# A 128-row slot for one expert's last block that is at most half full; its outputs computed, scaled and scattered in two parts of columns

## The chip, the core and the metric

The kernel runs on one NeuronCore of one Trainium2 chip, with its five engines: TensorE (PE; its weight loads are listed apart as PEld), VectorE (DVE), ScalarE (ACT), GpSimd (POOL) and SyncE (SP, which here issues DMAs). The metric is the time of one execution on the device in microseconds; lower is better. Before the change three runs took 935.01, 935.73 and 935.83 us, a median of 935.73 us.

## What is computed

Attention over 8 batches, 8 heads, 576 positions and 64 features, then a mixture of 8 experts in which each of the 4608 tokens goes to exactly one expert:

```python
q_rot, k_rot = rotate(q), rotate(k)
attn = softmax(q_rot @ k_rot.T / sqrt(D))
x = (attn @ v).transpose(0, 2, 1, 3).reshape(4608, 512)

logits = x @ w_gate + modality_bias[modality_id]
e_idx = argmax(logits, axis=1)
gate_w = softmax(logits)[arange(N), e_idx]
for e in range(8):
    mask = e_idx == e
    h = relu(x[mask] @ w1[e])                    # w1[e]: 512 x 1024
    out[mask] = gate_w[mask, None] * (h @ w2[e]) # w2[e]: 1024 x 512
```

Which token goes where depends on the data. For the inputs of the reference the experts get 0, 1143, 0, 0, 0, 0, 2289 and 1176 tokens. In blocks of 256 that is 4 full blocks and 119 tokens for expert 1, 8 full blocks and 241 tokens for expert 6, 4 full blocks and 152 tokens for expert 7.

## The kernel before

The first half of the program is attention: 32 pairs of heads, software-pipelined by a table of times (`KEYS`, `AT`). After each batch the router (`route`) finds each token's expert and its place in that expert's list, and `scatter` writes token number and gate weight into a table in DRAM (`TAB`), 4608 rows for each expert and one empty region behind them. Rows that nobody writes hold the number `EMPTY`, which every later gather and scatter skips as out of bounds.

The second half works through **slots**. A slot is one block of 256 rows of one expert's list. Slots 0 to 7 hold full blocks found after five batches (`plan0`, into `PLA`); 11 more (`NB_STATIC`), slots 8 to 18, are planned after the last batch (`plan`, into `PLB`). In both plans entry 0 of a slot is the expert, entry 1 the first row in `TAB`, entry 2 whether the expert differs from that of the slot before. `plan` counts the blocks that remain for each expert (`nb`), and writes their sum to `TOT`. Behind the static slots stands `tc.If(tot > NB_STATIC)`, whose body runs all the other slots up to `NB_MAX` = 17; a run in which 11 slots are enough skips it.

For the inputs here the blocks stand as follows: slots 0 and 1 are expert 1, slots 2 to 6 expert 6, slot 7 expert 7, slots 8 to 10 expert 1 (slot 10 is the block with 119 tokens), slots 11 to 14 expert 6, slots 15 to 18 expert 7 (slot 18 is the block with 152 tokens). `nb` is 3, 4 and 4, so `TOT` is 11.

What one slot does, in the order in which `chain` writes it for PE, DVE, ACT and POOL, which keep that order:

- `m_plan`, `m_ix` (three slots ahead): SP reads the slot's plan entries into registers and loads the table's rows twice, as `ix` (for scatter and scale) and `xi` (for the gather).
- `m_rows` (two slots ahead): POOL works out `iy` and issues eight indirect DMAs, which gather the rows of x into `XG`; `t` is the half of the rows, `g` a quarter of the features.
- `m_load1`, `m_load2` (one slot ahead): SP loads w1 and w2 of the slot's expert into `ST1` and `ST2`, 2 MB each in four DMAs of 512 KB. They are conditional: where the expert doesn't change, nothing moves.
- `m_split`: ACT rounds a quarter of the weights to fp32r (`W1H`, `W2H`), DVE takes what is left over (`W1L`, `W2L`). This is done for every slot, loaded or not.
- `m_tr`, `m_tre`: DVE transposes the gathered rows in 32 by 32 blocks, ACT and DVE split them into `XTH` and `XTL` (both are parts of `HL`).
- `m_l1`: 96 matmuls of 256 columns in four groups, each followed by `m_l1e`: ACT's relu gives the high part `hh`, DVE the low part `hl`.
- `m_l2(s, t)`, once for each half of the rows: 24 matmuls of 512 columns into one PSUM bank, ACT scales them into `y` (two buffers), and POOL scatters the 128 rows of `y` to the output.

The last batch's routing and `plan` itself run inside the chain: `one()` takes one item from the list `late`, and is called ten times in a slot (four times behind the groups of `m_l1e`, twice behind `m_tre`, four times behind `m_split`), six times in slot 0. With 14 steps of `route`, 5 scatters and 7 items of `plan` with four steps each, the list ends with slot 2.

The scatters all write the tensor `out`, so the program makes each of them wait until the one before has landed.

Of the kernel before, what the change touches and what calls it, by code (L numbers as in the profile page):

```python
# [8 lines left out]
F32 = mybir.dt.float32  # L9
# [9 lines left out]
P = 128  # L19
# [6 lines left out]
NB_STATIC = 11  # L26
# [59 lines left out]
def tile_attention_moe(ctx: ExitStack, tc: tile.TileContext, qk, v, mod, wg, mb, w1, w2, rope, cf, ci, out):  # L86
# [19 lines left out]
    PLB = cst.tile([1, 3, NB_MAX], I32, name="PLB")  # L106
# [507 lines left out]
    def plan():  # L614
# [19 lines left out]
        t88 = t1("t88", [E, E])  # L634
        V_.tensor_tensor(t88, tri, nb.unsqueeze(1).to_broadcast([1, E, E]), op=ALU.mult)
# [20 lines left out]
        V_.tensor_scalar(pl[:, 2, 0:ns], ch, 0.0, None, op0=ALU.not_equal)  # L656
        yield
# [45 lines left out]
    slots = [(0, i) for i in range(NA)] + [(1, i) for i in range(NB_MAX)]  # L703
# [10 lines left out]
    def m_ix(s):  # L714
        d = ms[s]
        ix = d["ix"] = ixp.tile([P, 2, 2], I32, name="ix", tag="ix")
        i1 = nc.sync.dma_start(out=ix, in_=TAB[bass.ds(d["r"], BLK), :].rearrange("(p t) w -> p t w", t=2)).ins
# [12 lines left out]
    def m_gather(s, t, g, after=None):  # L730
        d = ms[s]
        if "iy" not in d:
            d["iy"] = ixp.tile([P, 8], I32, name="iy", tag="iy")
            nc.gpsimd.tensor_scalar(d["iy"], d["xi"][:, :, 0], 4.0, cview("I4"), op0=ALU.mult, op1=ALU.add)
        rows = (N if slots[s][0] else NPL * S) * 4
        inst = nc.gpsimd.indirect_dma_start(out=XG[s % 2][:, t, g, :], out_offset=None,  # L736
                                            in_=X.rearrange("n (i f) -> (n i) f", f=P)[0:rows],
                                            in_offset=bass.IndirectOffsetOnAxis(ap=d["iy"][:, 2 * g + t:2 * g + t + 1], axis=0),
                                            bounds_check=rows - 1, oob_is_err=False)
# [65 lines left out]
    def m_l1e(s, g):  # L805
        d = ms[s]
        ps = d["ps", g]
        sl = slice(g * 2, g * 2 + 2)
        nc.scalar.activation(d["hh"][:, sl, :], ps, AF.Relu)
        nc.vector.scalar_tensor_tensor(d["hl"][:, sl, :], ps, 0.0, d["hh"][:, sl, :].bitcast(F32), op0=ALU.max, op1=ALU.subtract)  # L810

    def m_l2(s, t):
        d = ms[s]
        ps = bank("Y")
        m = 0
        for c in range(8):
            for hx, w in ((d["hh"], W2[0]), (d["hl"], W2[0]), (d["hh"], W2[1])):
                nc.tensor.matmul(ps, hx[:, c, t * P:(t + 1) * P], w[:, c, :], start=(m == 0), stop=(m == 23))  # L818
                m += 1
        y = yp.tile([P, DM], F32, name="y", tag="y")  # L820
        nc.scalar.activation(y, ps, AF.Copy, scale=d["ix"][:, t, 1:2].bitcast(F32))  # L821
        nc.gpsimd.indirect_dma_start(out=out, out_offset=bass.IndirectOffsetOnAxis(ap=d["ix"][:, t, 0:1], axis=0),  # L822
                                     in_=y, in_offset=None, bounds_check=N - 1, oob_is_err=False)
# [37 lines left out]
    for n in range(NPAIR):  # L861
# [34 lines left out]
        if n % 4 == 3:  # L896
# [75 lines left out]
    def chain(lo, hi, begun):  # L972
# [6 lines left out]
        for s in range(lo, hi):  # L979
# [17 lines left out]
            if nxt:  # L997
                for t in range(2):
                    m_tr(s + 1, t)
                for t in range(2):  # L1000
# [11 lines left out]
            m_l2(s, 1)  # L1012
# [6 lines left out]
    ns = NA + NB_STATIC  # L1019
# [3 lines left out]
    with tc.If(tot > NB_STATIC):  # L1023
        prefetch(ns)
        chain(ns, NA + NB_MAX, False)
# [100 lines left out]
```

## Time and profile before

| | |
|---|---|
| median of three runs | 935.73 us |
| the profiled execution, its own time | 935.48 us |
| its span (first to last instruction) | 933.7 us |
| mean granted TensorE clock | 0.998 |
| SP issues the last batch's rows of x to DRAM (the end of attention) | 499.18 us |
| period of one slot (ACT's scaling of slot 17 at 902.76 us, of slot 16 at 880.31 us) | 22.45 us |

The page of a profile lists for each engine how long it was busy, then groups of equal instructions with their number and the mean time of one. The timeline lists instructions in order of time: start, duration, engine, line of the code, operation, output and input. What stands in brackets is how long the engine had been idle before, and whose end released it by the profile's inference. The stretches view gives each engine's busy time and the DMA rate between two times. All times count from the start of the span.

### The profile page before, as it was taken

Reading aid. Unit: us, or ns where it says so; the run is one execution under the profiler, and the core shown is the slowest. Engines: PE = TensorE matmul, PEld = TensorE weight load, DVE = VectorE, ACT = ScalarE, POOL = GpSimd, SP = SyncE. Lnnn points to the kernel's source line nnn. Section 1 sums busy time; section 2 is a strip of 40 time slices with the busy share of each in tenths; the row PEclk is TensorE's granted clock in tenths of the full one; section 3 lists DMA queues with packets and bytes.
Section 4 is the critical chain, followed back from the end, with each engine's and each line's share of the span. In section 5 each row is a group of like instructions: output and inputs, shape, how many; then the busy total and the mean of one; then the engine's idle time right before and its main releaser. Section 6 shows DMA issues by size and latency. Waiting matters only on the chain. (4 is left out here: it accounts for less than half of the span.)

```text
span 933.7 us, 24945 instructions
## 1 busy us (share of the span) xinstructions
PE 899.7 (96%) x9248; PEld 739.8 (79%) x9248; DVE 670.0 (72%) x1165; ACT 629.5 (67%) x1292; POOL 664.9 (71%) x498
## 2 busy tenths in 40 slices
PE   2999999999999999999999999999999999999996
PEld 2777777777777777777778888898889999999995
DVE  7577787777877778777886778666666666666661
ACT  2778787787878778787884665665555666665651
POOL 3988879898898988999933877776655666666400
PEclk9999999999999999999999999999999999999999
DMA  8856857677676775766752721117712511251100
GB/s 264 237 171 186 227 156 199 197 182 215 169 200 197 184 218 159 205 179 187 209 157 75 209 64 36 51 62 235 231 46 72 195 41 55 92 180 46 37 24 17
DMA packets 79292, 136.90 MB, mean 147 GB/s; under 512 B 28699, under 2 KB 50603, under 8 KB 78140
## 3 DMA queue, kind: packets, MB, share of 16 engines
q1 hardware_dynamic: 68460, 114.06, 43.5%
q0 software_dynamic: 9440, 19.46, 6.4%
q10 hardware_dynamic: 1264, 1.72, 0.6%
q8 instruction: 75, 1.23, 0.6%
q14 instruction: 53, 0.43, 0.2%
HBM read 140.59 MB, written 19.77 MB: 172 GB/s over the span
## 5 line engine op out<-in xcount | busy, mean ns | idle before, releaser
L330 ACT ACTIVATE P<-ps,mn 128x576 f32<-128x576 f32 x288 | 210.4, 737 | 91.2 <-DVE mn L323 91.0
L323 DVE TENSOR_REDUCE mn<-ps 128x1 f32<-128x576 f32 x288 | 204.0, 745 | 93.0 <-PE ps L314 52.7
L736 POOL DMA_INDIRECT XG<-X,iy x152 | 186.4, 1226 | 66.8 <-issue 49.7
L801 PE MATMUL psH<-HL,W1H 128*128 128x256 f32 x1152 | 204.1, 280 | 0.0
L314 PE MATMUL ps<-SW 64*128 64x288 f32 x960 | 166.8, 314 | 15.5 <-DMA SW<-HL 15.4
L801 PEld LDWEIGHTS psH<-HL,W1H 128*128 128x128 f32 x1152 | 177.3, 188 | 1.9 <-ACT W1H L274 0.5
L314 PE MATMUL ps<-HL 64*128 64x288 f32 x960 | 166.6, 313 | 0.9 <-ACT P L330 0.8
L801 PE MATMUL psH<-HL,W1L 128*128 128x256 f32 x576 | 161.6, 281 | 1.4 <-DVE W1L L271 1.4
L314 PEld LDWEIGHTS ps<-SW 64*128 64x128 f32 x960 | 134.9, 190 | 26.9 <-DMA SW<-HL 15.0
L314 PEld LDWEIGHTS ps<-HL 64*128 64x128 f32 x960 | 137.1, 190 | 22.2 <-issue 12.8
L271 DVE TENSOR_TENSOR W1L<-ST,W1H 128x1024 fp32r<-128x1024 f32 x76 | 90.2, 1223 | 80.2 <-ACT W1H L274 80.2
L392 PE MATMUL pa<-PH,V 128*64 128x320 f32 (+1 forms) x1024 | 138.3, 412 | 0.0
L822 POOL DMA_INDIRECT out_dram<-y,ix x38 | 40.5, 1067 | 126.1 <-ACT y L821 103.1
L818 PE MATMUL psY<-W2H,SW 128*128 128x512 f32 x304 | 121.2, 399 | 0.0
L818 PE MATMUL psY<-W2L,SW 128*128 128x512 f32 x304 | 119.8, 394 | 0.0
L336 PE MATMUL ps<-idf,P 64*128 64x64 f32 x2624 | 105.8, 230 | 7.3 <-ACT P L330 1.8
L336 PEld LDWEIGHTS ps<-idf,P 64*128 64x128 f32 x2624 | 92.9, 141 | 22.3 <-ACT PH L274 9.0
L801 PEld LDWEIGHTS psH<-HL,W1L 128*128 128x128 f32 x576 | 108.4, 188 | 1.8 <-DVE W1L L271 1.8
L291 POOL TENSOR_TENSOR HL<-ST,HL 128x1216 fp32r<-128x1216 f32 x31 | 86.1, 2776 | 32.7 <-ACT HL L274 32.5
L392 PEld LDWEIGHTS pa<-PH,V 128*64 128x64 f32 x1024 | 67.9, 136 | 48.4 <-issue 10.0
L368 DVE COPY PH<-ps 128x512 f32<-128x512 f32 (+1 forms) x160 | 96.1, 633 | 8.6 <-PE ps L336 8.0
L271 DVE TENSOR_TENSOR W2L<-ST,W2H 128x1024 fp32r<-128x1024 f32 x76 | 92.6, 1219 | 4.5 <-ACT W2H L274 4.4
(173 smaller groups left out, 1585.4 us busy)
## 6 DMA issues: line engine op xcount, KB each, us to landing
ST<-in_moe_w_dram SPq DMA_DIRECT2D x152, 512.0 KB
ST<-in_qk_dram SPq DMA_DIRECT2D x62, 608.0 KB
SW<-HL SPq DMA_DIRECT2D x124, 232.0 KB
V<-in_v_dram SPq DMA_DIRECT2D x32, 256.0 KB
X<-X SPq DMA_DIRECT2D x8, 1024.0 KB
XG<-X,iy POOLq DMA_INDIRECT x152, 3.2
V<-in_v_dram SPq DMA_DIRECT2D x64, 16.0 KB
X<-XT SPq DMA_DIRECT2D x16, 64.0 KB
```

What stands on the lines that cost most here:

```text
L271: nc.vector.tensor_tensor(o, a, b, op=ALU.subtract)
L291: e.tensor_tensor(d["HL"][:, 1, c], a, d["HL"][:, 0, c].bitcast(F32), op=ALU.subtract)
L314: free(nc.tensor.matmul(ps[:, g, 0:288], t[:, wq, q0:q0 + P], t[:, wk, k0:k0 + 288], start=(m == 0), stop=(m == len(L) - 1)), seen)
L323: lastmin[d["ring", u]] = nc.vector.tensor_reduce(mn, d["S", u][:, :, 0:288], op=ALU.min, axis=AX.XY).ins
L330: nc.scalar.activation(p.rearrange("p (a b) -> p a b", a=2), ps[:, :, 0:288], AF.Exp, bias=d.pop(("m", u)), scale=-1.0, accum_out=d["sum"] ...
L336: free(nc.tensor.transpose(ps[0][:, g, c:c + 64], src[r, k0:k0 + P], idf[r, r]), ps[1])
L368: mine.append((nc.vector.tensor_copy if g else acopy)(o, i).ins)
L392: i = nc.tensor.matmul(pa[hh * 64:hh * 64 + 64, 0:c1 - c0], d["V"][:, hh, kt, :], r, start=(kt == 0), stop=(kt == 4))
L736: inst = nc.gpsimd.indirect_dma_start(out=XG[s % 2][:, t, g, :], out_offset=None, in_=X.rearrange("n (i f) -> (n i) f", f=P)[0:rows], in_o ...
L801: l1_[s] = nc.tensor.matmul(ps[:, i, :], w[:, c, f0:f0 + P], x[:, c, :], start=(m == 0), stop=(m == 11)).ins
L818: nc.tensor.matmul(ps, hx[:, c, t * P:(t + 1) * P], w[:, c, :], start=(m == 0), stop=(m == 23))
L822: nc.gpsimd.indirect_dma_start(out=out, out_offset=bass.IndirectOffsetOnAxis(ap=d["ix"][:, t, 0:1], axis=0), in_=y, in_offset=None, bounds ...
```

## The change

One of the eleven later slots is replaced by a slot of 128 rows. `plan` looks for the first expert whose last block has at most 128 tokens, takes that block out of its `nb`, and writes its place into an 18th entry of `PLB`. If there is none, that entry points at the table's empty region. The short slot stands behind the first ten later slots and in front of the `If`, whose bound becomes 10. The number of static slots is 19 as before. For the inputs here slots 8 and 9 are now expert 1, 10 to 13 expert 6, 14 to 17 expert 7, and slot 18 is the short one, with the 119 tokens of expert 1.

In the short slot only the first half of the rows (`t` = 0) is gathered, transposed and split; `m_l1` still runs with 256 columns, of which the second 128 are left from slot 17 and aren't used; `m_l1e` evaluates 128 columns. `m_l2` runs once, in two parts of 256 columns each with 24 matmuls; each part has its own PSUM bank, its own `y` and its own scatter into half rows of `out`, at row numbers `ho` that POOL works out ahead. `late` gets 13 items of `plan` in place of 7. The weights of the short slot, and of the slot that follows it in the `If`, are always loaded.

```diff
-NB_STATIC = 11
+NB_STATIC = 10
...
+    PLB = cst.tile([1, 3, NB_MAX + 1], I32, name="PLB")
...
+        V_.tensor_scalar(ni, nf, float(BLK // 2 - 1), None, op0=ALU.add)
...
+        V_.tensor_tensor(hm, nb, hm, op=ALU.subtract)
...
+        V_.tensor_scalar(hc, hc, 1.0, None, op0=ALU.is_equal)
...
+        V_.tensor_tensor(nb, nb, hm, op=ALU.subtract)
...
+        V_.tensor_copy(pl[:, 1, ns:ns + 1], hr)
...
+        V_.tensor_copy(pl[:, 0, ns:ns + 1], hr)
...
+        V_.memset(pl[:, 2, ns:ns + 1], 1)
...
+        V_.memset(pl[:, 2, NB_STATIC:NB_STATIC + 1], 1)
...
+    slots = [(0, i) for i in range(NA)] + [(1, i) for i in range(NB_STATIC)] + [(2, NB_MAX)] + [(1, i) for i in range(NB_STATIC, NB_MAX)]
+    halves = lambda s: range(1 if slots[s][0] == 2 else 2)
...
+            n = 4 * len(halves(s))
+            nc.gpsimd.tensor_scalar(d["iy"][:, 0:n], d["xi"][:, 0:n, 0], 4.0, cview("I4"), op0=ALU.mult, op1=ALU.add)
+            if n == 4:
+                ho = d["ho"] = ixp.tile([P, 2], I32, name="ho", tag="ho", bufs=1)
+                for h in range(2):
+                    nc.gpsimd.tensor_scalar(ho[:, h:h + 1], d["ix"][:, 0, 0:1], 2.0, float(h), op0=ALU.mult, op1=ALU.add)
...
-        for t in range(2):
+        for t in halves(s):
...
+        n = P * len(halves(s))
+        hh, hl = (d[x][:, g * 2:g * 2 + 2, 0:n] for x in ("hh", "hl"))
+        nc.scalar.activation(hh, ps[:, :, 0:n], AF.Relu)
...
+        nh = 2 if slots[s][0] == 2 else 1
+        w = DM // nh
+        for h in range(nh):
+            ps = bank("Y")[:, 0:w]
...
+                    nc.tensor.matmul(ps, hx[:, c, t * P:(t + 1) * P], x[:, c, h * w:h * w + w], start=(m == 0), stop=(m == 23))
...
+            nc.scalar.activation(y[:, 0:w], ps, AF.Copy, scale=gate)
+            row = d["ho"][:, h:h + 1] if nh > 1 else d["ix"][:, t, 0:1]
+            nc.gpsimd.indirect_dma_start(out=out.rearrange("n (i f) -> (n i) f", f=w) if nh > 1 else out,
...
-                late = steps + scats + [(each, next) + ((g, None),) * 4] * 7
+                late = steps + scats + [(each, next) + ((g, None),) * 4] * 13
...
-            m_l2(s, 1)
+            if len(halves(s)) > 1:
+                m_l2(s, 1)
...
-    ns = NA + NB_STATIC
+    ns = NA + NB_STATIC + 1
```

Two places in the order of instructions matter below. The first is the end of POOL's program in front of the `If`: the scatters of slot 17 (first two rows) and of slot 18, with the semaphores that each waits for. `DMASW`, with a number, is one of eight semaphores that count landed DMAs of POOL, taken in turn. Before:

```order
L822 DMA out_0_dram<-y_13269,ix_12433 4608x512 [waits DMASW7_49,DMAHW0_49,DMASW0_49,Activation_49]
L822 DMA out_0_dram<-y_13303,ix_12433 4608x512 [waits DMASW1_49,DMASW0_49,Activation_49]
L822 DMA out_0_dram<-y_13453,ix_12688 4608x512 [waits DMASW2_49,DMAHW2_49,DMASW1_49,Activation_49]
L822 DMA out_0_dram<-y_13483,ix_12688 4608x512 [waits DMASW3_49,DMASW2_49,Activation_49]
L1022 TENSOR_LOAD TOT_79 [waits DVE_49]
L1023 COMPARE_AND_BRANCH
```

And now, with the two half-row scatters (9216 rows of 256) in the third and fourth row:

```order
L895 DMA out_0_dram<-y_13284,ix_12460 4608x512 [waits DMAHW0_49,DMASW3_49,Activation_49]
L895 DMA out_0_dram<-y_13318,ix_12460 4608x512 [waits DMASW4_49,Activation_49]
L895 DMA out_0_dram<-y_13468,ho_12919 9216x256 [waits DMASW5_49,DMASW6_49,Activation_49,Pool_49]
L895 DMA out_0_dram<-y_13498,ho_12919 9216x256 [waits DMASW6_49,DMASW7_49,Activation_49,Pool_49]
L1097 TENSOR_LOAD TOT_79 [waits DVE_49]
L1098 COMPARE_AND_BRANCH
```

Each scatter still waits for the semaphore of the scatter before it: the second half's wait for `DMASW6` is for the landing of the first half.

The second place is DVE in slot 3, from the third group of the first layer to the transposes for slot 4 (`HL_82` is `hl`). Before:

```order
L271 TENSOR_TENSOR W2L<-ST_74,W2H 128x1024 [waits DMAHW0_49,Activation_49]
L810 SCALAR_TENSOR_TENSOR HL_82<-psH,SW_84 128x512 [waits Activation_49]
L271 TENSOR_TENSOR W2L<-ST_74,W2H 128x1024 [waits DMAHW1_49,Activation_49]
L810 SCALAR_TENSOR_TENSOR HL_82<-psH,SW_84 128x512 [waits Activation_49]
L781 STREAM_TRANSPOSE XG_75<-XG_75 128x512 [waits DMASW2_49,DMASW7_49,DMASW1_49,DMASW0_49]
```

And now:

```order
L877 SCALAR_TENSOR_TENSOR HL_82<-psH,SW_84 128x512 [waits Activation_49]
L709 MEMSET PLB 1x1 [waits DVE_49]
L714 TENSOR_SCALAR ge<-nb 1x8
L717 TENSOR_SCALAR fa<-AB 1x8
L719 TENSOR_TENSOR ge<-ge,fa 1x8 [waits DVE_49]
L271 TENSOR_TENSOR W2L<-ST_74,W2H 128x1024 [waits DMAHW1_49,Activation_49]
L877 SCALAR_TENSOR_TENSOR HL_82<-psH,SW_84 128x512 [waits Activation_49]
L721 TENSOR_TENSOR ge<-ge,fa 1x7 [waits DVE_49]
L723 TENSOR_TENSOR cmp<-cmp,ge 1x136 [waits DVE_49]
L726 TENSOR_REDUCE rb<-cmp 1x17 [waits DVE_49]
L729 TENSOR_SCALAR r_9773<-CF 1x17
L847 STREAM_TRANSPOSE XG_75<-XG_75 128x512 [waits DMASW2_49,DMASW7_49,DMASW1_49,DMASW0_49]
```

The rest of `plan` follows six items of `late` later than before: its old places in slot 2, between the parts of `W1L`, are taken by the new instructions on the short block, and behind the groups of slot 3 stand 22 small instructions where there were none (5, 5, 4 and 4 behind the four `hl`, 4 behind the transposes).

More of the change, by code (lines that the diff above doesn't have):

```diff
@@ L105, in tile_attention_moe @@
     PLA = cst.tile([1, 3, NB_MAX], I32, name="PLA")
-    PLB = cst.tile([1, 3, NB_MAX], I32, name="PLB")
+    PLB = cst.tile([1, 3, NB_MAX + 1], I32, name="PLB")
     TOT = cst.tile([1, 1], I32, name="TOT")
@@ L656, in plan @@
         V_.tensor_scalar(pl[:, 2, 0:ns], ch, 0.0, None, op0=ALU.not_equal)
+        yield
+        V_.memset(pl[:, 2, NB_STATIC:NB_STATIC + 1], 1)
         yield
@@ L701, in bank @@
         return spare.pop()
-    slots = [(0, i) for i in range(NA)] + [(1, i) for i in range(NB_MAX)]
+    slots = [(0, i) for i in range(NA)] + [(1, i) for i in range(NB_STATIC)] + [(2, NB_MAX)] + [(1, i) for i in range(NB_STATIC, NB_MAX)]
+    halves = lambda s: range(1 if slots[s][0] == 2 else 2)
     ms = {}
@@ L716, in m_ix @@
         ix = d["ix"] = ixp.tile([P, 2, 2], I32, name="ix", tag="ix")
+        if slots[s][0] == 2:
+            nc.sync.dma_start(out=ix[:, 0, :], in_=TAB[bass.ds(d["r"], P), :])
+            xi = d["xi"] = ixp.tile([P, 8, 2], I32, name="xi", tag="xi")
+            nc.sync.dma_start(out=xi[:, 0:4, :], in_=TAB[bass.ds(d["r"], P), :].rearrange("(q g) w -> q (g w)", g=4).unsqueeze(0).to_broadcast([4, 32, 8]))
+            return
         i1 = nc.sync.dma_start(out=ix, in_=TAB[bass.ds(d["r"], BLK), :].rearrange("(p t) w -> p t w", t=2)).ins
@@ L997, in chain @@
             if nxt:
-                for t in range(2):
+                for t in halves(s + 1):
                     m_tr(s + 1, t)
-                for t in range(2):
+                for t in halves(s + 1):
                     m_tre(s + 1, t)
@@ L1024, in tile_attention_moe @@
         prefetch(ns)
-        chain(ns, NA + NB_MAX, False)
+        chain(ns, len(slots), False)
 CF_OFF = {}
```

68 lines of the change are left out of this document (53 added, 15 removed).

## Prediction, made before the result was known

> **What bounds the kernel now.** I read the page first, then the stretches of the last two slots, then the timeline of their engines.
>
> ```profile
> span 933.7 us, 24945 instructions
> PE 899.7 (96%) x9248; PEld 739.8 (79%) x9248; DVE 670.0 (72%) x1165; ACT 629.5 (67%) x1292; POOL 664.9 (71%) x498
> ```
>
> ```profile
> 880.30:902.70 22.40, 22.40 (x146) 20.23 (x145) 15.26 (x16) 13.29 (x16) 1.96 (x2) 1.00 0.07 25
> 902.70:925.10 22.40, 22.40 (x144) 19.91 (x143) 9.58 (x10) 9.34 (x12) 1.95 (x2) 1.00 0.06 21
> ```
>
> In slots 17 and 18 (columns behind the stretch: its length, then PE, PEld, DVE, ACT, POOL busy, clock, DMA share, GB/s) PE is busy for all 22.4 us, at full granted clock (1.00), while the others rest a third of the time or more. But a busy PE isn't yet a price, because matmuls overlap. The price is the distance between starts. PE in slot 18, first and last matmul of each layer:
>
> ```profile
> 902.51 0.28 PE L801 MATMUL psH<-HL,W1H 128*128 128x256 f32 x1
> ...
> 913.66 0.28 PE L801 MATMUL psH<-HL,W1L 128*128 128x256 f32 x1
> 913.77 0.39 PE L818 MATMUL psY<-W2H,SW 128*128 128x512 f32 x1
> ...
> 924.73 0.40 PE L818 MATMUL psY<-W2L,SW 128*128 128x512 f32 x1
> ```
>
> The 96 matmuls of 256 columns take (913.66 - 902.51) / 95 = 0.1174 us each, the 48 of 512 columns (924.73 - 913.77) / 47 = 0.2332 us. So time goes by columns: half as many cost half. Behind the last matmul only a tail remains:
>
> ```profile
> 925.22 0.69 ACT L821 ACTIVATE y<-psY,ix 128x512 f32<-128x512 f32 x1 [4.92 <-PE psY L818]
> 926.18 0.97 POOL L822 DMA_INDIRECT out_dram<-y,ix  x1 [4.63 <-ACT y L821]
> ```
>
> ACT starts 0.49 us behind the last matmul's start, POOL 0.27 us behind ACT's end (925.91); POOL ends at 927.15, and landing, branch and the program's end take the 6.55 us to 933.7. So what ends last is PE, then this tail.
>
> **The change, part by part.**
>
> *Does the short slot get used?* Only if one of the experts leaves at most 128 rows. Counted from the reference, expert 1 leaves 119. The trace agrees: both scatters of slot 10 (from 741.23 and 746.55 us) and the last of slot 18 show, in the DMA view of their stretches:
>
> ```profile
> q0 software_dynamic: 80, 0.12, 6.7%
> ...
> q0 software_dynamic: 80, 0.12, 6.6%
> ...
> q0 software_dynamic: 80, 0.16, 5.2%
> ```
>
> 0.12 MB is 60 rows of 2 KB in each half, 119 or 120 in the block; 0.16 MB is 76 and so 152. `TOT` becomes 10, the bound is 10, and the body of the `If` stays skipped.
>
> *Layer 2 of the last slot.* Two parts of 24 matmuls with 256 columns. The operands have the shape of those in layer 1, so I take 0.1174 us. From the start at 913.77, the last matmul of part 0 starts at 913.77 + 23 x 0.1174 = 916.47, that of part 1 at 913.77 + 47 x 0.1174 = 919.29, against 924.73: **-5.44 us**. Part 0's `hl` isn't late either. DVE's last one, at the old size:
>
> ```profile
> 914.60 0.69 DVE L810 SCALAR_TENSOR_TENSOR HX<-psH,SW 128x512 fp32r<-128x512 f32 x1 [0.64 <-ACT SW L809]
> ```
>
> It is done at 915.29, and now it is half as wide; its first user, the 20th matmul of part 0, starts at 913.77 + 19 x 0.1174 = 916.00.
>
> *Scale.* 128x256 from PSUM by the same ACT operation:
>
> ```profile
> L274 ACT ACTIVATE oT<-pa 128x256 f32<-128x256 f32 x32 | 12.2, 382 | 0.1
> ```
>
> 0.38 us in place of 0.69. The 0.49 us from a matmul's start to ACT shrinks with the matmul's shown time (0.40 to 0.28), to 0.37. Part 0 is scaled from 916.84 to 917.22, part 1 from 919.66 to 920.04: a further -0.43 us.
>
> *Scatters.* POOL could take part 0 at 917.49 (till 918.46) and part 1 at 920.31. But part 1 waits for the landing of part 0. The nearest rows are those where y had long been ready: slot 4's second y, scattered in the last row below.
>
> ```profile
> 610.87 0.69 ACT L821 ACTIVATE y<-psY,ix 128x512 f32<-128x512 f32 x1 [3.02 <-PE psY L818]
> ...
> 618.94 1.45 POOL L822 DMA_INDIRECT out_dram<-y,ix  x1 [0.30 <-issue]
> 622.91 0.99 POOL L822 DMA_INDIRECT out_dram<-y,ix  x1 [2.53 <-ACT SW L809]
> ...
> 635.68 1.41 POOL L822 DMA_INDIRECT out_dram<-y,ix  x1 [0.30 <-issue]
> 641.78 1.03 POOL L822 DMA_INDIRECT out_dram<-y,ix  x1 [4.69 <-DVE HX L810]
> ```
>
> y was done at 611.56, POOL stood idle for 2.53 us, so the named ACT instruction isn't the cause; the landing is. In the second pair, while weights are loading, it is 4.69 us. At the end of the kernel DMA is quiet (21 GB/s above), so I take 2.53: part 1 starts at 918.46 + 2.53 = 920.99 and not at 920.31, **+0.68 us**. Bounds: 0 (landing in time) and +2.84 us (4.69). What waits behind it is only POOL's load of `TOT`, the branch and the end. Ending at 920.99 + 0.97 = 921.96, plus 6.55 us, the span is 928.51.
>
> The Trainium skill ("DMA: Bandwidth & Descriptors", Anatomy of one DMA) gives a POOL DMA about 2.0 us of fixed time, mostly the receipt of the write, plus bytes over 436 GB/s. It speaks against cutting one output in two, since here the fixed part is paid in series. By it part 0 (0.12 MB) would land 2.28 us after its issue, and part 1 would start at 920.74: 0.25 us earlier than by the row.
>
> *New work on DVE in slot 3.* PE needs `hl` there in time: the fourth one when its 20th matmul of layer 2 starts (last row).
>
> ```profile
> 565.37 0.15 DVE L668 TENSOR_TENSOR ge<-ge,fa 1x7 f32<-1x7 f32 x1
> 565.55 0.29 DVE L670 TENSOR_TENSOR cmp<-cmp,ge 1x136 f32<-1x136 f32 x1
> 565.87 0.28 DVE L673 TENSOR_REDUCE rb<-cmp 1x17 f32<-1x136 f32 x1
> 566.08 0.21 DVE L676 TENSOR_SCALAR r<-CF 1x17 f32<-1x17 f32 x1
> ```
>
> ```profile
> 571.63 0.67 DVE L810 SCALAR_TENSOR_TENSOR HL<-psH,SW 128x512 fp32r<-128x512 f32 x1
> ...
> 575.94 1.23 DVE L271 TENSOR_TENSOR W2L<-ST,W2H 128x1024 fp32r<-128x1024 f32 x1 [0.16 <-ACT W2H L274]
> 577.80 0.69 DVE L810 SCALAR_TENSOR_TENSOR HL<-psH,SW 128x512 fp32r<-128x512 f32 x1 [0.64 <-ACT SW L809]
> ```
>
> ```profile
> 581.40 0.39 PE L818 MATMUL psY<-W2H,HL 128*128 128x512 f32 x1
> ```
>
> 14 small instructions now stand between the first `hl` and the fourth. They start 0.18 to 0.32 us apart, some 0.2 on average: 2.8 us, less 0.80 us of idle time that they fill, so the fourth `hl` ends at 578.49 + 2.0 = 580.5, before 581.40: cost **nothing**, with 0.9 us to spare. At 0.32 each it ends at 582.2, 0.8 us late; that is the upper bound, and nothing behind it (transposes, `XTL`, `W1L`) has less room.
>
> *A sixth set of weights.* Slot 18 now loads expert 1's 4.2 MB, which slot 18 of before didn't. The nearest case is slot 15, loaded from 810.27; DMA by stretches (last column GB/s):
>
> ```profile
> 810.27 7.11 SPq L752 DMA_DIRECT2D ST<-in_moe_w_dram  x4
> ...
> 877.63 6.80 SPq L752 DMA_DIRECT2D ST<-in_moe_w_dram  x4
> ```
>
> ```profile
> 815.00:820.00 5.00, 5.00 (x45) 5.00 (x45) 5.00 (x6) 4.38 (x6) 4.42 (x3) 1.00 0.76 249
> 820.00:825.00 5.00, 5.00 (x41) 4.83 (x40) 3.71 (x5) 2.22 (x4) 4.08 (x4) 1.00 0.94 297
> 825.00:830.00 5.00, 5.00 (x23) 4.02 (x22) 3.78 (x5) 2.07 (x2) 3.39 (x4) 1.00 0.77 259
> 830.00:835.00 5.00, 5.00 (x23) 4.02 (x22) 2.36 (x2) 2.58 (x3) 1.01 (x1) 1.00 0.18 64
> ```
>
> All of it has landed some 20 us after the first issue, w1, issued first, in the first half of that, and PE never waited. For slot 18 that is 877.6 to 898. ACT first reads the two here:
>
> ```profile
> 897.75 2.00 ACT L274 ACTIVATE W1H<-ST 128x1024 fp32r<-128x1024 f32 x2
> ...
> 905.24 1.05 ACT L274 ACTIVATE W2H<-ST 128x1024 fp32r<-128x1024 f32 x1
> ```
>
> That is 20 us behind the first issue for w1 and 28 us for w2. Cost: **nothing**. If it were late, PE would wait for the whole of it beyond the some 2 us that lie between the split of w1's first quarter and 902.51.
>
> *Dropped with the second half:* four gathers, one transpose, one split in slots 16 and 17, all beside a busy PE: nothing. The two `ho` and the narrower `iy` stand on POOL in slot 16 in place of four gathers of 1.0 us or more.
>
> **Sum**: -5.44 - 0.43 + 0.68 = -5.19 us, from 935.48 (profiled execution; the runs' median is 0.25 higher) to **930.3 us**. For comparison: one part of 512 columns would give -24 x 0.2332 = -5.60 us, so cutting in two loses 0.4 us as I see it.
>
> **Rivals.**
>
> 1. *The second scatter doesn't wait*, since part 0 lands by 920.3. For it: smaller rows. Against: 2.53 us was the least in a quiet stretch. Time 929.6. Chance 0.10.
> 2. *The small DVE instructions hold up PE* in slot 3 by up to 0.8 us: 931.1. For it: DVE has next to no gap between the first `hl` and the fourth. Against: 0.9 us of room. Chance 0.08.
> 3. *Narrow matmuls are bound by their weight loads.* Each load takes 188 ns:
>
> ```profile
> L801 PEld LDWEIGHTS psH<-HL,W1H 128*128 128x128 f32 x1152 | 177.3, 188 | 1.9 <-ACT W1H L274 0.5
> ```
>
> If loads came one after the other, part 1's last matmul would start at 913.77 + 47 x 0.188 = 922.61, POOL would end at 924.60, and the time would be 932.9. Against: layer 1 has the same loads and runs at 0.117. The Trainium skill ("TensorE: Matmul & The Clock Gate", Back-to-back issue gap) says that in a stream of pairs of load and matmul the spacing is set by both, 81 ns at 128 columns and 131 ns at 512, so that half the columns is not half the time. An estimate on the line between its two figures is 98 ns at 256 columns, three quarters of 131, by which layer 2 here would save a quarter of 11.2 us, 2.8 us, and not 5.4. The trace disagrees: 117 against 233 ns. Chance 0.03.
>
> 4. *Slower: the `If` is taken.* It decides at 128 tokens: with 129 in the last block of expert 1 no short block is found, `TOT` stays 11, and 11 > 10 sends the program through all seven slots of the body, 7 x 22.4 = 157 us, behind a load of w1 that nothing hides (some 10 us): about 1097. Against: 119, from two sides. Chance 0.02.
> 5. *No change*: w1 of slot 18 lands some 27 us after its issue (20 to ACT's read, 2 of room, 5.2 that eat up the gain) in place of 20 or less: 935.5. Against: PE's busy share of 22.40 in 22.40 us in slots behind such loads. Chance 0.03; 0.01 for worse.
>
> **How the numbers follow.** The forecast has 0.73: 930.3. The range takes in rivals 1 and 2 and most of the scatter's bounds: 929.2 to 932.4. A measurement can tell about 0.2%, 1.9 us, from no change: faster 0.94 (forecast and rivals 1 to 3), same 0.03, slower 0.03.
>
> **What would show it.** Right: 48 matmuls of 256 columns 0.117 us apart in the last slot; two scatters of about 1 us with POOL idle some 2.5 us between them, the second y done 0.7 us before the second scatter; PE without idle time from slot 3 on. Wrong: idle PE around 581 us (rival 2) or in front of slot 18's matmuls (5); a spacing near 0.19 (3); work behind the branch (4).

## The result and the profile after

| kernel | us, median (runs, range) | ratio to before, 95% interval |
|---|---|---|
| before | 935.37 (4, 934.90 to 935.83) | |
| after | 928.76 (4, 927.24 to 931.42) | 0.9925 [0.9906, 0.9943] |
| forecast | 930.3 (929.2 to 932.4) | 0.9945 |

The change makes the kernel 6.6 us faster; 5.2 were forecast, and the median lies 0.4 us below the range. The profiled execution of after took 931.42 us (span 929.5), the slowest of its four. First the page of after and the stretches of slots 17 and 18 (columns as before):

```profile
span 929.5 us, 24955 instructions
PE 891.4 (96%) x9248; PEld 733.8 (79%) x9248; DVE 672.8 (72%) x1187; ACT 626.9 (67%) x1291; POOL 664.3 (71%) x496
```

```profile
880.90:903.30 22.40, 22.40 (x146) 20.22 (x145) 13.64 (x14) 12.34 (x15) 1.95 (x2) 1.00 0.59 192
903.30:920.50 17.20, 17.20 (x146) 16.96 (x144) 8.55 (x10) 8.27 (x12) 1.93 (x2) 1.00 0.03 11
```

PE is busy in all of 17.20 us of the short slot, where slot 18 of before had 22.40, and the sixth set of weights (192 GB/s in slot 17) costs it nothing. The timeline of after's end, in three pieces, from slot 17's second scaling; then first and last matmul of layer 2:

```profile
903.71 0.69 ACT L893 ACTIVATE y<-psY,ix 128x512 f32<-128x512 f32 x1 [3.01 <-issue]
917.75 0.47 ACT L893 ACTIVATE y<-psY,ix 128x256 f32<-128x256 f32 x1 [2.50 <-PE psY L890]
920.60 0.47 ACT L893 ACTIVATE y<-psY,ix 128x256 f32<-128x256 f32 x1 [2.37 <-PE psY L890]
```

```profile
918.99 0.97 POOL L895 DMA_INDIRECT out_dram<-y,ho  x1 [13.35 <-ACT y L893]
922.80 0.97 POOL L895 DMA_INDIRECT out_dram<-y,ho  x1 [2.84 <-DMA out_dram<-y,ho]
```

```profile
914.66 0.28 PE L890 MATMUL psY<-W2H,SW 128*128 128x256 f32 x1
...
920.23 0.28 PE L890 MATMUL psY<-W2L,SW 128*128 128x256 f32 x1
```

The 48 matmuls stand (920.23 - 914.66) / 47 = 0.1185 us apart (forecast 0.1174). The first scatter starts 0.77 us behind its scaling (917.75 + 0.47 to 918.99), where 0.27 was forecast, and the second waits for the landing. The chain of waits shows how (start, duration, what; POOLq is POOL's sequencer):

```profile
918.99 2.95 DMA out_dram<-y,ho
...
921.97 0.02 POOLq L895
921.99 0.04 issue
922.03 0.04 POOLq L895
922.07 0.52 issue
922.59 0.50 POOLq L1097
```

The landing takes 2.95 us from the first scatter's start. Two short entries of POOL's sequencer follow (921.97, 922.03), and then 0.52 us in which, as we read it, the second scatter is set up.

Where the rest came from is seen further ahead. First matmul of layer 2 in slots 0, 2, 4 and 17, before and then after:

```profile
506.89 0.39 PE L818 MATMUL psY<-W2H,SW 128*128 128x512 f32 x1
...
554.52 0.39 PE L818 MATMUL psY<-W2H,SW 128*128 128x512 f32 x1
...
599.43 0.39 PE L818 MATMUL psY<-W2H,SW 128*128 128x512 f32 x1
...
891.32 0.39 PE L818 MATMUL psY<-W2H,SW 128*128 128x512 f32 x1
```

```profile
509.57 0.40 PE L890 MATMUL psY<-W2H,SW 128*128 128x512 f32 x1
...
556.27 0.40 PE L890 MATMUL psY<-W2H,SW 128*128 128x512 f32 x1
...
601.07 0.40 PE L890 MATMUL psY<-W2H,SW 128*128 128x512 f32 x1
...
892.26 0.40 PE L890 MATMUL psY<-W2H,SW 128*128 128x512 f32 x1
```

From slot 4 to slot 17 before takes 291.89 us, after 291.19: 22.45 and 22.40 us a slot, though PE runs the same instructions there and waits for nothing. From slot 0 to slot 4 before takes 92.54, after 91.50. Neither was in the forecast. Against it, slot 0's layer 2 starts 2.68 us later in this execution; in ten profiles taken on the first chips, of either kernel, that start lies anywhere from 506.4 to 510.0 us, so a single execution says little of a change of 1 us.

The chips of the last two batches were slower for all kernels (before took 940 to 945 us there), and single executions stalled at odd places, so from those runs only distances within one stage are compared, and the ratios (not the medians) of small_pad and after_dense leave out one slow run each.

### The profile page after: what moved, and what is told of

Read it like the earlier page. It is cut to its first block, busy times and chain, and to the rows that moved or that the text cites. A ratio compares the mean times of both kernels' runs of the same rounds, so it can differ in the third digit from the quotient of the medians.

```text
span 929.5 us, 24955 instructions
## 1 busy us (share of the span) xinstructions
PE 891.4 (96%) x9248; PEld 733.8 (79%) x9248; DVE 672.8 (72%) x1187; ACT 626.9 (67%) x1291; POOL 664.3 (71%) x496
## 4 chain that ended last, share of the span: by engine, by line
PE 65%; ACT 15%; DVE 8%; issue 6%; DMA 2%; POOL 2%; SPq 1%; DVEq 0%; POOLq 0%; ACTq 0%
PE psH L867 20%; PE psY L890 20%; ACT P L330 13%; PE ps L314 11%; PE pa L392 8%; DVE mn L323 6%; PE ps L336 6%; ACT PH L274 1%; POOL XG L802 1%; DMA SW<-HL 1%; DMA XG<-X,iy 1%; DVE ST L287 1%; DMA ST<-in_qk_dram 0%; PE pa L424 0%; DMA out_dram<-y,ho 0%
## 5 line engine op out<-in xcount | busy, mean ns | idle before, releaser
L895 POOL DMA_INDIRECT out_dram<-y,ix x36 | 44.5, 1236 | 105.1 <-ACT y L893 58.1
L890 PE MATMUL psY<-W2H,SW 128*128 128x512 f32 (+1 forms) x304 | 118.8, 391 | 0.0
L890 PE MATMUL psY<-W2L,SW 128*128 128x512 f32 (+1 forms) x304 | 118.2, 389 | 0.0
L271 DVE TENSOR_TENSOR W2L<-ST,W2H 128x1024 fp32r<-128x1024 f32 x76 | 92.5, 1218 | 4.7 <-ACT W2H L274 4.6
```

What stands on the lines that cost most here:

```text
L271: nc.vector.tensor_tensor(o, a, b, op=ALU.subtract)
L890: nc.tensor.matmul(ps, hx[:, c, t * P:(t + 1) * P], x[:, c, h * w:h * w + w], start=(m == 0), stop=(m == 23))
L895: nc.gpsimd.indirect_dma_start(out=out.rearrange("n (i f) -> (n i) f", f=w) if nh > 1 else out, out_offset=bass.IndirectOffsetOnAxis(ap=ro ...
```

## The experiments

In this table "0 to 4" and "4 to 17" are the distances of the layer-2 starts of those slots, "end" the distance from slot 17's second scaling to the end of the trace, all in us from the profiled execution; the time is the median.

| kernel | time | ratio to before | 0 to 4 | 4 to 17 | end |
|---|---|---|---|---|---|
| before | 935.37 | | 92.5 | 291.9 | 30.9 |
| before_again | 936.06 | 0.9999 [0.9983, 1.0014] | 92.3 | 292.0 | 30.9 |
| after | 928.76 | 0.9925 [0.9906, 0.9943] | 91.5 | 291.2 | 25.8 |
| after_again | 929.92 | 0.9934 [0.9911, 0.9957] | 91.6 | 291.2 | 26.2 |
| one_part | 929.55 | 0.9928 [0.9901, 0.9954] | 91.4 | 291.2 | 24.6 |
| parts_nowait | 929.43 | 0.9933 [0.9915, 0.9952] | 91.7 | 291.2 | 26.2 |
| pad128 | 936.05 | 0.9985 [0.9971, 1.0000] | 92.8 | 291.2 | 31.2 |
| after_unshift | 931.73 | 0.9943 [0.9922, 0.9963] | 91.9 | 291.9 | 26.5 |
| one_narrow | 928.57 | 0.9905 [0.9885, 0.9925] | 91.5 | 291.2 | 24.1 |

**The same kernels again.**

> The kernel before, unchanged, for the spread of one kernel and for the parts of its span. Theory A (the size of the gain lies in the start): attention begins 1.7 to 2.9 us earlier or later from one execution to the next, whatever the kernel, so the time against the other copy of the kernel before is within 0.3%, the period of a slot is 22.45 us as in the first profile, and the start (27th exponential, 41.81 us before) may differ by 1 to 3 us. Theory B (the change makes the expert stage itself faster): the period is again 22.45 us and the first slots are as before, within 0.1 us.

> The changed kernel, unchanged. Theory A: ratio 0.9925 to 0.9945 to the kernel before (5 to 7 us faster); from the end of slot 17 on the profile repeats the first one of this kernel (second scatter 3.8 us after the first, 0.7 us or more of it waiting), the 27th exponential is earlier than 43.55 us, and the slots' period follows the chip, so that it equals that of the copy of the kernel before run beside it. Theory B: the period is 22.40 us again while the copy of the kernel before has 22.45 us, and slots 1 to 3 take 1 us less.

The end (30.9 against 25.8 and 26.2) and the slot period come out the same each time: after_again has 22.40 us where before_again, on the same chip, has 22.45, so theory B holds for the period, and theory A's guess that it follows the chip falls. Theory B's "first slots as before, within 0.1 us" was missed: from slot 0 to slot 2 the same kernel took 47.6 us in before and 46.9 in before_again. The time itself spreads by 4 to 6 us among executions of one kernel; the median of after_again, 929.92 us, lies inside the forecast range. What a part of the change is worth is therefore read from distances inside the profile.

**The place of the weights.** The change adds four small tiles (`hm`, `hc`, `hr`, `ho`). In the program's layout they push `W1H`, `W1L`, `W2L` and `y` 128 bytes higher. pad128 does that to before, after_unshift undoes it in after; no instruction is added or taken away:

```diff
-full = t1("full", [E, NB_MAX])[:, :, 0:most]
+full = t1("full", [E, NB_MAX + 4])[:, :, 0:most]   # pad128, in before
+full = t1("full", [E, NB_MAX - 4])[:, :, 0:most]   # after_unshift, in after
```

> The kernel before; only a scratch tile of plan0 (full) is made 128 bytes longer, so that W1H, W1L, W2L and y lie 128 bytes higher in SBUF, as they do in the changed kernel. No instruction is added. Place theory (the slot period fell from 22.45 to 22.40 us because these tiles moved): slot period 22.40 us, layer 1 at 116.7 ns a matmul, some 0.05 us less in each of 15 slots, 0.8 us in all. Rival (the period fell with the changed instructions): 22.45 us, 117.3 ns, no change of the time.

> The changed kernel; the same scratch tile is made 128 bytes shorter, so that W1H, W1L, W2L and y lie where they lie in the kernel before. Place theory: slot period back to 22.45 us, layer 1 at 117.3 ns, the time 0.8 us above that of the changed kernel, at about 930.7 us. Rival: 22.40 us as in the changed kernel.

Layer 2 of slots 4 and 17 in pad128, then in after_unshift:

```profile
602.84 0.39 PE L818 MATMUL psY<-W2H,SW 128*128 128x512 f32 x1
...
894.03 0.40 PE L818 MATMUL psY<-W2H,SW 128*128 128x512 f32 x1
```

```profile
598.24 0.39 PE L890 MATMUL psY<-W2H,SW 128*128 128x512 f32 x1
...
890.13 0.39 PE L890 MATMUL psY<-W2H,SW 128*128 128x512 f32 x1
```

291.19 and 291.89 us: pad128 has the period of after, after_unshift that of before. The place theory holds, and the rival falls; the times (ratio 0.9985 for pad128, 931.73 us where 930.7 was expected for after_unshift) are too wide to tell 0.8 us. Between 600 and 890 us the matmuls of layer 1 stand 116.7 ns apart on average in pad128 and after, 117.3 in before and after_unshift. Two more places show that this is no rule of "higher is better":

```diff
-full = t1("full", [E, NB_MAX])[:, :, 0:most]
+full = t1("full", [E, NB_MAX + 2])[:, :, 0:most]   # pad64; + 8 in pad256
```

> The kernel before with its scratch tile 64 bytes longer: W1H, W1L, W2L and y 64 bytes higher. If the spacing goes by the place in small steps, the slot period lies between 22.40 and 22.45 us; if only some places are bad, it is one of the two. Nothing else changes.

> The kernel before with its scratch tile 256 bytes longer: W1H, W1L, W2L and y 256 bytes higher. If the place counts modulo 256 bytes, the slot period is 22.45 us as before; if not, 22.40 or another value.

```profile
607.93 0.40 PE L818 MATMUL psY<-W2H,SW 128*128 128x512 f32 x1
...
903.08 0.40 PE L818 MATMUL psY<-W2H,SW 128*128 128x512 f32 x1
```

That is pad64: 295.15 / 13 = 22.70 us a slot, layer 1 at 119.9 ns, 0.25 us a slot worse than before. pad256 has a period of 22.45 again between slots that don't wait, so the place counts modulo 256 bytes as far as these four places tell. Why it counts, and for which of the moved tiles, isn't shown.

**One part, or two without the wait.** one_part sets `nh = 1`; parts_nowait takes the second scatter's wait for the first one's landing away (the two write different columns):

```diff
-nh = 2 if slots[s][0] == 2 else 1
+nh = 1                                              # one_part
...
+if h:
+    tc.declare_no_dep(inst, part0, reason="other columns")   # parts_nowait
```

> The changed kernel with layer 2 of the short slot in one part of 512 columns: 24 matmuls, one scaling of 128x512, one scatter of whole rows. By the sum of the prediction the cut into two parts costs 0.4 us; by the first profile of the changed kernel, in which the second scatter waited 1.46 us instead of 0.68, it costs about 0.9 us more or less: from last matmul's start to the end of the span about 8.97 us as before the change (924.73 to 933.7), last matmul 24 x 0.233 us after the layer's start. Expected 0.3 to 1.2 us less than the changed kernel. If the parts gain instead (the rival), it is 0.4 us or more slower.

> The changed kernel, with the second part's scatter no longer ordered behind the landing of the first (they write different columns). If that wait is what the two parts pay for, POOL issues the second scatter 0.27 us after its scaling ends, with idle time set by ACT and not by a DMA, and the span ends 0.7 to 1.5 us earlier than in the changed kernel; if the landing of the second is what ends the program whatever its issue, it gains under 0.3 us.

one_part's end:

```profile
900.98 0.69 ACT L893 ACTIVATE y<-psY,ix 128x512 f32<-128x512 f32 x1 [3.01 <-issue]
917.78 0.69 ACT L893 ACTIVATE y<-psY,ix 128x512 f32<-128x512 f32 x1 [5.26 <-PEq L1098]
```

```profile
918.74 0.97 POOL L895 DMA_INDIRECT out_dram<-y,ix  x1 [15.83 <-ACT y L893]
```

Its scatter starts 0.27 us behind the scaling, and its end takes 24.6 us: two parts cost 1.2 to 1.6 us, and not 0.4. The times (929.55 and 929.92) can't tell that. In parts_nowait the second scatter doesn't wait for a landing:

```profile
920.07 0.47 ACT L893 ACTIVATE y<-psY,ix 128x256 f32<-128x256 f32 x1 [2.37 <-PE psY L890]
```

```profile
921.31 0.97 POOL L895 DMA_INDIRECT out_dram<-y,ho  x1 [1.88 <-issue]
```

It starts 0.77 us behind its scaling (0.27 expected), 1 us sooner than in after (922.80 - 921.07 = 1.73), yet the end is no shorter (0.7 to 1.5 us less were expected). The DMA view of two stretches shows what took the gain (packets, MB, share); the first ends at 923.8 us, the second begins at 924.3:

```profile
q0 software_dynamic: 45, 0.11, 28.6%
...
q0 software_dynamic: 3, 0.01, 4.6%
```

Three of the 48 packets came late, and the last landing stood 3.3 us behind POOL's end, against 2.0 in after. Single late packets are seen in before too (the scatter from 920.58 us landed 3.4 us behind POOL's end, that from 926.18 only 2.2), so whether the overlap caused it here stays open.

**Why 0.77 and not 0.27 us.** The half-row scatters take their row numbers from `ho`, which POOL writes, so they wait for POOL as well as for ACT and the DMAs. one_ho puts such an `ho` under one part of 512 columns; ho_act lets ACT write `ho` in after:

```diff
+nc.gpsimd.tensor_scalar(ho[:, h:h + 1], d["ix"][:, 0, 0:1], 1.0, 0.0, ...)           # one_ho
+row = d["ho"][:, h:h + 1] if "ho" in d else d["ix"][:, t, 0:1]                       # one_ho
-nc.gpsimd.tensor_scalar(ho[:, h:h + 1], d["ix"][:, 0, 0:1], 2.0, float(h), ...)
+nc.scalar.activation(ho[:, h:h + 1], d["ix"][:, 0, 0:1], AF.Copy, scale=2.0, bias=float(h))   # ho_act
```

> The one-part kernel, but its one scatter of 512 columns takes its row numbers from ho, written by POOL (the numbers of ix copied), as the scatters of the two-part kernel do. Theory of the extra wait (the wait for POOL's own ho pushes the wait for ACT out of the scatter into a semaphore instruction ahead of it, so that some 0.5 us of setting up the scatter no longer run while ACT scales): the scatter starts 0.77 us behind the end of the scaling, not 0.27. Rival (the narrow form of the scatter or of the scaling costs it): 0.27 us as in the one-part kernel.

> The changed kernel; the two ho are computed by ACT in place of POOL, so that the wait for ACT covers them. Theory of the extra wait: the first half-row scatter starts 0.27 us behind the end of its scaling (0.77 in the changed kernel), all behind it comes 0.5 us earlier, and from slot 17's second scaling to the end it takes 25.4 us (25.8 and 26.2 in the two profiles of the changed kernel). Rival (the narrow form costs it): 0.77 us and 25.8 to 26.2 us.

Scaling and first scatter, one_ho and then ho_act:

```profile
924.03 0.69 ACT L893 ACTIVATE y<-psY,ix 128x512 f32<-128x512 f32 x1 [5.26 <-PE psY L890]
...
925.48 0.97 POOL L895 DMA_INDIRECT out_dram<-y,ho  x1 [16.32 <-ACT y L893]
```

```profile
933.73 0.47 ACT L893 ACTIVATE y<-psY,ix 128x256 f32<-128x256 f32 x1 [2.50 <-PE psY L890]
...
934.48 0.97 POOL L895 DMA_INDIRECT out_dram<-y,ho  x1 [12.85 <-ACT y L893]
```

0.76 us with POOL's `ho` under full rows, 0.28 with ACT's under half rows: it is the extra wait, not the narrow form. The Trainium skill (Perfetto Trace Analysis, Identifying Dependency Chains) says that an instruction which waits for several engines may get semaphore instructions in front of it that carry the further waits. The trace agrees: two sequencer entries stand there at 921.97 and 922.03 above. That the 0.52 us behind them are set-up which otherwise runs while ACT scales is our reading; the runs show its price, 0.5 us. ho_act's end as a whole was missed: 26.8 us in place of 25.4, mostly because its first landing took 3.2 us from POOL's end (2.0 in after) and the second scatter waits for it. one_ho, ho_act, pad64 and pad256 are single executions (934.61, 948.27, 947.72 and 944.22 us, beside 940.29 for before on that chip); ho_act's slots 0 to 4 alone took 104.3 us, so its time says nothing of the edit.

**The hidden work alone.** extras adds to before only the change's other two loads: 23 small DVE instructions in `plan`, and slot 18's weights always loaded.

```diff
+for i in range(23):
+    V_.tensor_tensor(nf, EBv, AB, op=ALU.add)
+    yield
...
+V_.memset(pl[:, 2, NB_STATIC - 1:NB_STATIC], 1)
...
-late = steps + scats + [(each, next) + ((g, None),) * 4] * 7
+late = steps + scats + [(each, next) + ((g, None),) * 4] * 13
```

> The kernel before with two additions of the change alone: 23 more small DVE instructions in plan (their results are not used) with 13 items in the list, and slot 18's weights always loaded. As the prediction has it, both are hidden: no idle time of PE above 0.2 us in slots 2 to 4 or in front of slot 18's matmuls, slot period 22.45 us, end from slot 17's second scaling 30.9 us. Rival: PE idles up to 0.8 us around 581 us, or waits for w1 or w2 of slot 18.

All waits of PE from 500 to 930 us (whom it waited for, us in total, times, longest):

```profile
PE psH L806 <- DVE W1L L271: 1.4, 2, 0.8
```

Nothing stands in front of slot 18, its period is 22.45 us and its end takes 30.9 us as before: the weights are hidden. Its time, of a single execution, is 936.62 us, beside 937.22 for before on that chip. One wait of 0.75 us (at 589.47) is above the 0.2 expected, but pad128, which has neither addition, has the same one (0.76 us), so the additions aren't its cause.

**Slots 0 to 4.** That wait led to the last question. In three profiles of kernels with the old list of 7 `plan` items (before, before_again, pad128) slots 0 to 4 take 92.3 to 92.8 us, in the six of after and its variants in the table above 91.4 to 91.9. But extras, which has before's slots and the new list of 13 items, takes 93.2. POOL's gathers in slot 2, here with DVE's large instructions beside them, before and then after:

```profile
569.37 1.20 DVE L271 TENSOR_TENSOR W1L<-ST,W1H 128x1024 fp32r<-128x1024 f32 x1
570.03 2.55 POOL L736 DMA_INDIRECT XG<-X,iy  x1 [0.30 <-issue]
570.50 1.21 DVE L271 TENSOR_TENSOR W2L<-ST,W2H 128x1024 fp32r<-128x1024 f32 x1
571.63 0.67 DVE L810 SCALAR_TENSOR_TENSOR HL<-psH,SW 128x512 fp32r<-128x512 f32 x1
572.24 1.20 DVE L271 TENSOR_TENSOR W2L<-ST,W2H 128x1024 fp32r<-128x1024 f32 x1
```

```profile
571.02 1.23 DVE L271 TENSOR_TENSOR W1L<-ST,W1H 128x1024 fp32r<-128x1024 f32 x1
571.78 1.33 POOL L802 DMA_INDIRECT XG<-X,iy  x1 [0.31 <-issue]
572.16 0.13 DVE L678 TENSOR_SCALAR hr<-hr 1x1 f32<-1x1 f32 x1
...
572.62 1.23 DVE L271 TENSOR_TENSOR W2L<-ST,W2H 128x1024 fp32r<-128x1024 f32 x1
```

Before, `plan` is done by now, DVE's large instructions follow each other, and a gather takes 2.55 us; in after, the longer `plan` puts small ones between them, and the gather takes 1.33. It adds up: from the seventh write to `TAB` behind attention to slot 2's first scatter POOL takes 20.7, 20.2 and 19.8 us in the three with the old list, 17.9 in all six of after and its variants, and 19.0 in extras. Behind the scatters hangs `y`, behind `y` ACT's split of the weights, and so PE could gain. The Trainium skill (SBUF — State Buffer, SBUF: two separate sides) has a rule that fits: a DVE instruction with two inputs in SBUF and a GpSimd one that reads SBUF share a pair of ports, and whoever has it keeps it for a whole instruction. No run here shows the ports themselves; three test what follows from the gaps. small_tail puts 24 small instructions behind before's `plan`, small_pad adds the 128 bytes, after_dense packs after's `plan` closer:

```diff
 V_.tensor_copy(TOT, cum[:, E - 1:E])
 yield
+for i in range(24):                                  # small_tail, small_pad
+    V_.tensor_scalar(nf, EBv, 1.0, None, op0=ALU.add)
+    yield
...
-[(each, next) + ((g, None),) * 4] * 13
+[(each, next) + ((g, None),) * 8] * 7                # after_dense
```

> The kernel before with 24 small DVE instructions behind the last step of plan (their results are not used) and 13 items in the list; plan itself stays where it was. Theory of gaps (DVE's large instructions hold up POOL, worst where they stand next to each other; small ones between them let POOL through): from the end of the seventh write to TAB behind attention to slot 2's first scatter 17.9 to 19 us (20.7, 20.2 and 19.8 in before, before_again and pad128; 17.9 in the changed kernels), and from slot 0's to slot 4's layer 2 91.8 us (92.5, 92.3, 92.8; 91.9 in after_unshift), so some 0.7 us less in all. Rival (the wide instructions of plan in slot 2 hold up POOL): about 20 us and 92.3 to 92.8 us as before.

> The same with the scratch tile of plan0 128 bytes longer, so both additions that don't belong to the short slot. If the two account for what the prediction left out, slot 0's layer 2 to slot 18's takes 405.2 us as in the changed kernel (405.1 and 405.2; 406.9 and 406.8 in the kernel before), and the time is some 1.7 us below before, ratio 0.998. If not, it stays near 406.4 as in pad128.

> The changed kernel with plan's steps in 7 items of eight steps in place of 13 of four, so that plan is done in slot 2 and no small instructions stand between DVE's large ones at its end and in slot 3. Theory of gaps: the stretch from the seventh write to TAB to slot 2's first scatter back to about 20 us, slot 0's to slot 4's layer 2 92 to 92.5 us where the changed kernel has 91.5, and the time up to 1 us above the changed kernel's. Rival (only the number of small instructions or the short slot itself counts): 17.9 us and 91.5 us.

In this table "POOL's stretch" is the one from the seventh `TAB` write to slot 2's first scatter, and the distance of slots 0 to 4 is cut at the start of slot 2's layer 2:

| kernel | POOL's stretch | 0 to 2 | 2 to 4 | 0 to 4 | time | ratio |
|---|---|---|---|---|---|---|
| before | 20.7 | 47.6 | 44.9 | 92.5 | | |
| before_again | 20.2 | 46.9 | 45.4 | 92.3 | | |
| pad128 | 19.8 | 46.7 | 46.1 | 92.8 | | |
| extras | 19.0 | 46.9 | 46.3 | 93.2 | | |
| after | 17.9 | 46.7 | 44.8 | 91.5 | | |
| small_tail | 18.2 | 46.3 | 44.9 | 91.2 | 944.57 | |
| small_pad | 17.6 | 50.4 | 45.3 | 95.8 | 942.93 | 0.996 [0.9922, 0.9998] |
| after_dense | 20.0 | 48.0 | 45.4 | 93.4 | 936.17 | 0.9874 [0.9804, 0.9944] |

POOL's stretch goes as the theory of gaps has it in all three: shorter with the small instructions though `plan`'s wide ones stay in slot 2, longer when they are packed. That PE gains by it isn't shown, and the traces speak against it. Layer 2 of slots 0 and 2 in small_tail, then the first instruction that only the edit has, on DVE, in after and in small_tail:

```profile
515.07 0.39 PE L821 MATMUL psY<-W2H,SW 128*128 128x512 f32 x1
...
561.40 0.39 PE L821 MATMUL psY<-W2H,SW 128*128 128x512 f32 x1
```

```profile
561.51 0.15 DVE L636 TENSOR_SCALAR ni<-nf 1x8 int32<-1x8 f32 x1
```

```profile
576.25 0.32 DVE L686 TENSOR_SCALAR nf<-CF 1x8 f32<-1x8 f32 x1
```

Up to the start of slot 2's layer 2, at 554.52 us in before and 556.27 in after, PE, DVE, ACT and POOL run the same instructions in the same order in both; only places differ. In that part alone before takes 47.63 us and after 46.70: 0.93 of the 1.04 us lie ahead of the first new instruction. PE waits there for `W1L` for 1.4 us in before, 1.1 in after, and 0.7 in before_again, which is the same kernel as before. From slot 2 to slot 4 before takes 44.90 us and after 44.80, which is no more than the 0.05 us a slot of the place. The lead of small_tail, 46.33 us up to slot 2, lies ahead of its first added instruction as well. Nor do the distances from slot 2 to slot 4 follow POOL's stretch: before has the longest stretch and loses nothing, while extras, with a shorter one, loses most, in the wait of 589.47 us. So small instructions shorten POOL's stretch, but what makes slots 0 to 4 longer in some executions stays open.

The other two decide little: up to slot 2 they took 1.3 us (after_dense) and 3.7 us (small_pad) more than after, and small_pad's distance of slots 0 to 18 (413.8, expected 405.2) is lost to stalls. Its time agrees with 1.7 us less, but also with no more than 0.2; that of after_dense is too wide to show a loss of 1 us.

**A narrower layer 1.** one_narrow is one_part with 128 columns in the short slot's layer 1:

```diff
-nc.tensor.matmul(ps[:, i, :], w[:, c, f0:f0 + P], x[:, c, :], ...)
+nc.tensor.matmul(ps[:, i, 0:n], w[:, c, f0:f0 + P], x[:, c, 0:n], ...)   # n = 128 in the short slot
```

> The changed kernel with layer 2 of the short slot in one part of 512 columns and layer 1 of the short slot with 128 columns in place of 256 (the second 128 aren't used). If matmuls go by columns down to 128, the 96 of layer 1 take 0.0585 us each and save 5.6 us against the one-part kernel: about 924.0 us. If weight loads set the spacing at 128 columns, they take 0.08 to 0.10 us each (an estimate from the Trainium skill, TensorE: Matmul & The Clock Gate, Back-to-back issue gap, 81 ns a pair at 128 columns) and save 2 to 3.5 us: 926 to 927.5. If the split of w2 on ACT and DVE becomes the bound of the last slot, PE idles between the layers and about 1 us of the saving is lost.

First and last matmul of that layer, then the group of its weight loads (in the stretch of the slot):

```profile
903.47 0.33 PE L868 MATMUL psH<-HL,W1H 128*128 128x128 f32 x2
...
914.02 0.27 PE L868 MATMUL psH<-HL,W1L 128*128 128x128 f32 x1
```

```profile
L868 PEld LDWEIGHTS psH<-HL,W1H 128*128 128x128 f32 x63 | 9.6, 192 | 0.0
```

(914.02 - 903.47) / 95 = 0.111 us each: half the columns save 5%, and the end only 0.5 us (24.1), where 5.6 or 2 to 3.5 us were expected. The spacing here is set by something that doesn't shrink with the columns; the weight loads, one for each matmul, are the likely thing, but no run here tests them. The Trainium skill (TensorE: Matmul & The Clock Gate, Back-to-back issue gap) has 81 ns for such a pair at 128 columns; the trace's 111 decides.

## Why the prediction fell short

The sum on record, from the profiled executions of before and after. The sum had no term for the slots ahead of the last one, so they stand with 0:

| term | forecast | measured | how |
|---|---|---|---|
| layer 2 of the last slot | -5.44 | -5.45 | (920.23 - 903.71) - (924.73 - 902.76) |
| ACT | -0.43 | -0.34 | last matmul to end of scaling: 0.84 against 1.18; scaling took 0.47, not 0.38 |
| second scatter | +0.68 | +1.46 | scaling to scatter: 1.73 against 0.27 |
| behind the last scatter | 0 | -0.77 | 5.78 against 6.55 |
| the end | -5.19 | -5.10 | |
| slots 4 to 17 | 0 | -0.70 | 291.19 against 291.89 |
| slots 0 to 4 | 0 | -1.04 | 91.50 against 92.54 |

- **The mechanism was right.** PE bounds the last slot, layer 2 goes by columns, and the last slot's term came out to 0.01 us (0.06 of its 5.45 us fell in layer 1, with the place of the tiles; layer 2 alone gave 5.39). That the end as a whole came out so close (5.10 against 5.19; 4.7 in after_again) is luck: the second scatter cost 0.78 us more than forecast and the tail 0.77 us less.
- **The step that failed** is the sum's silence on the slots ahead of the last one. The prediction asked whether new work could hold up PE, and put everything there at nothing; that the four new tiles push the weight tiles 128 bytes further wasn't considered. pad128 and after_unshift show what it is worth: 0.05 us a slot, -0.70 us from slot 4 to slot 17 and about -0.2 (an estimate, four times 0.05) from slot 0 to slot 4. With that term the forecast would have been 929.4 us, and the range, which reached down by 1.1 us, would have held the 928.76.
- **What stays open** is the rest of slots 0 to 4, some 0.8 us. 0.93 of the 1.04 us passed before the two kernels' instructions differ, so it is no gain of the new instructions; the same kernel before differs by 0.7 us in that part from one profile to the next. The parts behind attention make -6.8 us together in this pair of profiles and -6.3 in the second, beside the 6.6 measured; the medians of the second pair lie 5.4 us apart.
- **The two-part cost was mis-sized**: 0.4 forecast, 1.2 to 1.6 measured against one_part. The wait for the landing was foreseen with about its size (2.84 us of idle POOL, 2.53 forecast); the 0.5 us that the wait for `ho` costs were not, though the order of POOL's waits on record showed the extra one. Of the tail's 0.77 us less, 0.54 lie behind the last landing: from there to the end of the trace it takes 3.79 us in after, after_again and parts_nowait, and 4.33 in before, before_again, pad128 and extras. Why is not shown.
- **Rivals.** The scatter waits (1 falls). The small DVE instructions hold up nothing: after has no wait of PE around 581 us (2 falls). Narrow matmuls are not bound by their loads at 256 columns: they stand 0.1185 us apart, not 0.19 (3 falls). The branch isn't taken and w1 isn't late (4 and 5 fall).

## What to carry to other kernels

Where PE never waits, count the columns that go, and price what each new wait puts in front of a transfer: here half the output cost an extra half microsecond because a row number came from POOL itself. A few small tiles that push others along can be worth as much as an edit's own second term, so a range for a change of 0.6% needs room for that, on either side. To tell such parts from the spread of executions (4 to 6 us here), compare distances between the same instructions in the profiles, and move one thing at a time. Before a distance is put down to new instructions, look whether they stand inside it at all: here most of 1 us lay ahead of them.

## What was not expected of the hardware

- Moving the weight tiles by 64, 128 and 256 bytes changes the spacing of 256-column matmuls from 117.3 ns to 119.9, 116.7 and 117.5, with the same instructions and no wait on PE: 22.45 us a slot become 22.70, 22.40 and 22.45. (`y` moves along with them.)
- A gather's issue on POOL takes from 1.0 to 2.55 us. The stretch of eight gathers and three writes takes 20.7 us where DVE's large instructions follow each other, and 17.9 where small ones stand between them (18.2 in small_tail, 20.0 in after_dense); PE gained nothing by it that could be shown.
- Matmuls of 128 columns, each with its own weight load, follow each other every 111 ns, those of 256 every 117.
- A scatter's start behind the instruction that it waits for last is 0.27 us or 0.77, by one more engine among its waits.
